# A pair of MLP chunks by seven block products: another order of products and sums, weight mixing begun earlier, a late half of the last DFT, outputs in 128-row pieces

## Chip, cores and metric

One core of a Trainium2 chip runs the kernel. The metric is the device time of one execution in microseconds (us). TensorE (PE) multiplies, VectorE (DVE), ScalarE (ACT) and GpSimd (POOL) do elementwise work, and the queue of SyncE (SP) issues the DMAs. Each engine takes its instructions in program order.

## What is computed

```
x  = attention(q, k, v)          # 8 batches, 32 global rows + 512 local rows (window 32), 8 heads of 64
X  = fft(fft(x, axis=1), axis=2) # 544 rows, 512 columns
u  = x + real(X)
un = (u - mean(u)) / sqrt(var(u) + 1e-6)
y  = u + relu(un @ w_ch1) @ w_ch2     # 512 -> 2048 -> 512
```

Inputs and output are float32. Every float32 operand of a matmul is split into two float16 parts, hi and lo, and the three products hi·hi, hi·lo, lo·hi are summed, so each product of the mathematics is three matmuls on PE.

## The kernel before

**Stages.** The eight batches pass through attention, a DFT (`d_` functions: a first half along the rows, `d_first`, a second half `d_second` by three pieces kt = 0, 1, 2, whose last is the tail of 32 rows, `d_tailsec`; `d_addc`, `d_add`, `d_as`, `d_tadd` add the result to x) and an MLP (`f_` functions). The MLP works on 17 chunks of 256 rows; chunk 16 collects the eight 32-row tails. Chunks 0 to 12 run the plain way, each with 8 steps of `f_first` (first layer into PSUM), `f_hi` and `f_lo` (relu and its two float16 parts) and `f_second` (second layer, summed in PSUM).

**The two pairs.** The last four chunks run as two pairs u = 0 and 1, (13, 14) and (15, 16): `jobs_duo`. For the first layer of a pair the rows of the two chunks and two halves of the 512 inputs and of the hidden columns make 2 by 2 blocks, and seven block products P1 to P7 take the place of eight. The products need sums of blocks of the activations (`s_un`, `s_mix` on DVE, split by `s_hi` on ACT and `s_lo` on DVE, turned by a DMA transpose `s_turn`, groups g = 0 to 3) and sums of blocks of the weights, which POOL makes in eight pieces n (`t_sum` twice, `t_mix`, `t_lo`; `t_hi` is on ACT between the last two). A pair runs in two halves:

- first half, 8 steps s: P1 and P2. `p_copy` takes P1 from PSUM to SBUF (x1), `p_sum` makes c11 = P2 + x1, `p_relu` (ACT) and `p_rest` (DVE) split it, `p_second` multiplies it into the accumulator of the first chunk;
- second half, 8 steps s: P4, P5, P6, P7, P3. `p_copy` takes P4 and P5 to SBUF; then x1 = P6 + x1, u3 = P7 + x1, c12 = x1 + P5, c21 = u3 − P4, c22 = u3 + P5, c12 = P3 + c12, two `p_relu`, two `p_rest`, and two `p_second`: number 2 (c21 and c22, 12 matmuls of 512 columns, second chunk) and number 1 (c12, 6 matmuls, first chunk). PE runs the `p_second` of a step after the five products of the next one.

One product is 6 matmuls of 256 columns in one PSUM bank. Four banks (`bk`) are shared by the products, the DFT and the attention; P1 of the first pair goes to `ps1` instead.

**What sets the order.** `Plan.run` places every job by costs and due times (`add(engine, cost, function, ..., t=due)`) and picks the banks; the program is then emitted in that order, so costs and due times move instructions on all five queues. `T_AT` and `T_PACE` are the due time of weight piece 0 and the distance of the pieces; `BOOST` brings the DFT of the last batch forward by 40.

**Names in the rows.** Second half of a pair: `bk` is a product in PSUM; `msk`, `vN`, `xd`, `xk` hold x1, and `kT` holds u3 (in the first half c11), `ph` holds c12, c21 and c22, `h` and `hb` are the split operands of `p_second`, `un`, `et`, `pg`, `unh` belong to the `s_` functions, `pgr`, `vf`, `tf`, `tq`, `tp` to the `t_` functions, and `ug`, `pe`, `uh` are turned activations.

**End.** `f_end` adds the accumulator into the X tile, one 128-row piece j at a time, and `f_out` writes a chunk: chunks below 16 as one DMA of 256 rows, chunk 16 as two DMAs whose target is 4 by 32 rows.

## Time and profile before

| | us |
|---|---|
| median of 3 runs | 1039.15 (1038.97 to 1042.64) |
| profiled execution | 1041.4 |
| its span | 1039.6 |
| PE busy | 922.8 (89%) |
| DVE busy | 734.4 (71%) |
| ACT busy | 621.6 (60%) |
| POOL busy | 599.8 (58%) |

The profile counts microseconds from the start of the span. A share of busy time is an average over the stages; which engine bounds a stage is read from windows of the trace, from the waits of PE and from the chain of work that ended last. "granted clock" is TensorE's clock as a share of its upper level, 2.4 GHz; 0.50 is its lower level, 1.2 GHz. Mean durations overlap a little between neighbours of one engine: the distance from start to start of two equal DVE instructions is about 0.08 us less than the duration.

### The profile page before, as it was taken

To read this page: it belongs to the slowest core of one execution; us is meant where nothing else is said; L and a number is where in the kernel's file an instruction comes from. 1 tells how busy PE (TensorE), PEld (TensorE's weight loads), DVE (VectorE), ACT (ScalarE), POOL (GpSimd) and SP (SyncE) were. 2 spreads that over 40 slices of the span, in tenths; PEclk is the share of its full clock that TensorE was granted. 3 is DMA by queue.
4 is the path that set the end of the run, shared out by engine and by line. 5 is a ranking of instruction groups with operands and counts; after the bars stand their busy time and mean duration, and the time that the engine had idled before them with its cause. 6 is when DMAs were issued, how large, how long until landed. Compare 5 with 4: busy or idle time off the path is not lost.

```text
span 1039.6 us, 25360 instructions
## 1 busy us (share of the span) xinstructions
PE 922.8 (89%) x9768; PEld 640.7 (62%) x9768; DVE 734.4 (71%) x1929; ACT 621.6 (60%) x1379; POOL 599.8 (58%) x861
## 2 busy tenths in 40 slices
PE   2353558999999999999999999999999998799995
PEld 1243346666777677666766776677676775466662
DVE  4887998977668856785688568867755568984442
ACT  7996777972787388638864885578355334332221
POOL 6999765862686267526854784486246467850000
PEclk9986579999999999999999999999999999899998
DMA  9899356462675286329752874485245114121001
GB/s 361 252 281 239 91 107 135 108 135 42 146 149 116 40 173 133 87 44 170 142 107 55 143 164 75 88 159 94 40 85 79 42 31 85 21 52 41 1 1 41
DMA packets 227761, 113.10 MB, mean 109 GB/s; under 512 B 202776, under 2 KB 210104, under 8 KB 227640
## 3 DMA queue, kind: packets, MB, share of 16 engines
q1 hardware_dynamic: 227640, 111.49, 48.6%
q8 instruction: 76, 1.25, 0.5%
q14 instruction: 45, 0.37, 0.1%
HBM read 47.37 MB, written 9.44 MB: 55 GB/s over the span
## 4 chain that ended last, share of the span: by engine, by line
PE 61%; DVE 7%; DMA 4%; POOL 4%; ACT 3%; issue 1%; SPq 1%; DVEq 0%; POOLq 0%; ACTq 0%
PE ps L1059 20%; PE acc L1078 20%; PE bk L1207 4%; PE ps L1265 3%; PE bk L616 3%; PE acc L1265 2%; DMA pl<-ph 2%; PE bk L940 2%; PE bk L661 1%; PE bk L664 1%; DMA X<-xt 1%; PE bk L905 1%; PE bk L688 1%; PE bk L724 1%; DVE ph L1234 1%
## 5 line engine op out<-in xcount | busy, mean ns | idle before, releaser
L1059 PE MATMUL ps<-uh,wh 128*128 128x256 f16 x2496 | 290.3, 273 | 3.5 <-DVE h L1068 2.7
L1078 PE MATMUL acc<-wh,h 128*128 128x512 f16 x1248 | 286.5, 379 | 1.9 <-DVE h L1068 1.1
L1059 PEld LDWEIGHTS <-wh 128*128 128x128 f16 x2496 | 240.2, 98 | 38.7 <-issue 4.7
L1078 PEld LDWEIGHTS <-h 128*128 128x128 f16 x1248 | 116.3, 98 | 131.0 <-DVE h L1068 2.9
L640 POOL TENSOR_TENSOR ph<-pe,ph 128x448 f16<-128x448 f32 (+1 forms) x128 | 139.0, 1100 | 74.1 <-ACT ph L635 60.9
L1068 DVE SCALAR_TENSOR_TENSOR h<-ps,h 128x512 f16<-128x512 f32 x104 | 71.5, 688 | 117.2 <-ACT h L1064 117.0
L1064 ACT ACTIVATE h<-ps 128x512 f16<-128x512 f32 x104 | 61.5, 592 | 117.6 <-PE ps L1059 116.9
L624 DVE CUSTOM_DVE_ANT_0 pe<-bk,msk,z 128x224 f32<-128x224 f32 (+1 forms) x256 | 102.3, 454 | 19.6 <-PE bk L616 14.5
L631 ACT ACTIVATE pe<-pe,nm 128x224 f32<-128x224 f32 (+1 forms) x256 | 104.8, 475 | 13.0 <-DVE nm L624 12.7
L661 PE MATMUL bk<-vN,pl 128*128 128x65 f16 x768 | 66.5, 200 | 23.7 <-DMA pl<-ph 14.7
L635 ACT ACTIVATE ph<-pe 128x448 f16<-128x448 f32 (+1 forms) x128 | 70.9, 578 | 18.4 <-DMA pl<-ph 17.8
L661 PEld LDWEIGHTS <-pl 128*128 128x128 f16 x768 | 58.7, 103 | 26.0 <-DMA pl<-ph 20.8
L1039 POOL TENSOR_TENSOR ve<-ve 128x2 f32<-128x2 f32 x17 | 4.3, 251 | 102.5 <-DVE un L1019 99.9
L616 PEld LDWEIGHTS <-qT 64*128 64x128 f16 x1536 | 49.8, 98 | 21.4 <-issue 17.9
L664 PEld LDWEIGHTS <-pl 96*128 96x128 f16 (+1 forms) x768 | 56.9, 102 | 10.0 <-issue 6.0
L616 PE MATMUL bk<-kT,qT 64*128 64x192 f16 (+2 forms) x1536 | 57.0, 220 | 6.7 <-POOL kT L600 4.2
L664 PE MATMUL bk<-vB,pl 96*128 96x65 f16 (+1 forms) x576 | 50.9, 201 | 0.0
L1265 PE MATMUL acc<-wh,h 128*128 128x512 f16 x192 | 46.6, 379 | 1.6 <-ACT h L1247 1.0
L600 POOL TENSOR_TENSOR kT<-qk,kT 128x559 f16<-128x559 f32 x32 | 40.6, 1270 | 12.3 <-ACT kT L595 12.1
L431 PE MATMUL wl<-wm,partb 128*128 128x256 bf16 x64 | 18.4, 390 | 32.8 <-DVE wm L421 32.8
L575 POOL TENSOR_TENSOR vN<-vf,vN 128x640 f16<-128x640 f32 x32 | 44.5, 1393 | 4.3 <-ACT vN L571 4.0
L1265 PE MATMUL ps<-wh,hb 128*128 128x512 f16 x192 | 45.2, 385 | 1.2 <-DVE hb L1252 1.2
...
## 6 DMA issues: line engine op xcount, KB each, us to landing
...
pl<-ph SPq DMA_TRANSPOSE x128, 3.3
```

What stands on the lines that cost most here:

```text
L616: nc.tensor.matmul(S[h][:, t + w0:t + w1], qT[r, a, j], kT[r, k0:k0 + w1 - w0], start=m == 0, stop=m == 2)
L624: nc.vector.tensor_tensor_reduce(self.per[j][:, h, 0:w], S[h][:, t:t + w], self.msk[:, j, 0:w], z[:, 8:9], 3e38, op0=ALU.add, op1=ALU.min, ...
L631: self.nc.scalar.activation(pe[:, h], pe[:, h], AF.Exp, bias=nm[:, h:h + 1], scale=-1.0)
L635: self.nc.scalar.activation(ph[:, 0, :, 0:WIDE[i % 4]], self.per[i % 4][:, :, 0:WIDE[i % 4]], AF.Copy)
L640: self.nc.gpsimd.tensor_sub(ph[:, 1, :, 0:w], self.per[i % 4][:, :, 0:w], ph[:, 0, :, 0:w])
L661: nc.tensor.matmul(pv[:, j % 2, h], pl[:, 4 * a + 2 * h], vN[:, j, c, h, :], start=m == 0, stop=False)
L664: nc.tensor.matmul(pv[:, j % 2, h], pl[0:n, 4 * a + 2 * h + 1], vb, start=False, stop=m == 2)
L1059: nc.tensor.matmul(ps[:, q], wt[:, w, c0:c0 + P], uh[:, :, 4 * a + kt, :], start=n == 0, stop=n == 11)
L1064: self.nc.scalar.activation(h[:, 0], self.fps[c, fp], AF.Relu)
L1068: self.nc.vector.scalar_tensor_tensor(h[:, 1], self.fps.pop((c, fp)), 0.0, h[:, 0], op0=ALU.max, op1=ALU.subtract)
L1078: nc.tensor.matmul(self.acc_f[c][j], h[:, a, q, j * P:(j + 1) * P], self.w[1, f][:, w, :], start=f == 0 and a == 0 and w == 0, stop=f == 1 ...
L1265: nc.tensor.matmul(self.acc_f[c][j], h[:, a, q, j * P:(j + 1) * P], self.w[1, f][:, w, :], start=first and q + a + w == 0, stop=last and q ...
```

## The change

1. **Sums.** The order of products in the second half is P6, P7, P5, P4, P3 (for s = 7: P6, P7, P5, P3, P4). `p_copy` of P4 and P5 is gone: c12 = P5 + x1, c22 = P5 + u3 and c21 = u3 − P4 each take one operand from PSUM. In s = 7 `p_second` 1 stands before `p_second` 2.
2. **Weight pieces.** `T_AT` is 808 in place of 826, `T_PACE` 9.0 in place of 7.5; the planner's costs of `t_sum`, `t_mix`, `t_hi`, `t_lo` are larger.
3. **Last batch.** `BOOST` no longer holds for the second DFT half of pieces kt = 1 and 2 and what follows them (`d_second`, `d_addc`, `d_add` of kt = 1, `d_tailsec`, `d_as`, `d_tadd`).
4. **Outputs.** `p_out` writes the 128-row piece j of a chunk right after its `f_end`; chunk 16 keeps its two DMAs to 4 by 32 rows.
5. **Order of groups and costs.** For j = 1 the groups are made in the order 1, 2, 3 in place of 3, 1, 2; the planner's costs of `s_un`, `s_mix`, `s_lo`, `p_sum`, `p_rest`, `p_relu`, `d_addc`, `d_add` are larger.

No matmul is added or removed. The planner's order is the same on all queues until late in batch 7 (PE's row 15,729 of 19,466).

```diff
-T_AT, T_PACE = 826.0, 7.5
+T_AT, T_PACE = 808.0, 9.0
...
+    def p_out(self, c, j):
+        b, k = divmod(c, 2)
+        to = self.out[b, 256 * k + P * j:256 * k + P * j + P, :] if b < B else self.out[4 * j:4 * j + 4, SL:T, :]
+        self.nc.sync.dma_start(to, self.u_row(c, j))
...
     def p_copy(self, u, s, n):
-        self.nc.scalar.activation(self.p_bufs(s)[{"P1": "x1", "P4": "c21", "P5": "c22"}[n]], self.pb[u, s, n], AF.Copy)
+        self.nc.scalar.activation(self.p_bufs(s)["x1"], self.pb[u, s, n], AF.Copy)
...
-        (ve.tensor_sub if o == "c21" else ve.tensor_add)(v[o], a, v[b])
+        if o == "c21":
+            ve.tensor_sub(v[o], v[b], a)
+        else:
+            ve.tensor_add(v[o], a, v[b])
...
-            add("POOL", 2.6, self.t_mix, n, r=[("qT", "T", n, 0), ("qT", "T", n, 1)], w=[tw], t=T + 3)
-            add("ACT", 1.1, self.t_hi, n, r=[tw, *done.get(n, [])], w=[home], t=T + 5)
+            add("POOL", 3.4, self.t_mix, n, r=[("qT", "T", n, 0), ("qT", "T", n, 1)], w=[tw], t=T + 3)
+            add("ACT", 1.25, self.t_hi, n, r=[tw, *done.get(n, [])], w=[home], t=T + 5)
...
-            add("DVE", 1.35, self.s_mix, u, j, r=un, w=[mix, ("sm", 0)], t=L, back=False)
-            for g in (3, 1, 2):
+            add("DVE", 2.5, self.s_mix, u, j, r=un, w=[mix, ("sm", 0)], t=L, back=False)
+            for g in ((1, 2, 3) if j else (3, 1, 2)):
...
-            b = prod(s, "P4", t)
-            add("ACT", .36, self.p_copy, u, s, "P4", r=[b, *end], w=[cw, R], t=-1e3, back=False)
-            b = prod(s, "P5", t)
-            add("ACT", .36, self.p_copy, u, s, "P5", r=[b, *end], w=[cz], k=[R], t=-1e3, back=False)
             b = prod(s, "P6", t)
             summ(s, "x1", "P6", "x1", [b, x1], [x1], xk)
             b = prod(s, "P7", t)
-            summ(s, "u3", "P7", "x1", [b, x1], [u3, ("xu", u, s)], xk)
-            summ(s, "c12", "x1", "c22", [x1, cz], [c12], [R, *xk], .34)
-            b = prod(s, "P3", t)
-            summ(s, "c21", "u3", "c21", [u3, cw], [cw], [R, ("xu", u, s)], .34)
-            summ(s, "c22", "u3", "c22", [u3, cz], [cz], [R, ("xu", u, s)], .34)
-            split(s, 2, .58, [cw, cz], [R], ("pl", "s", u, s), [f, f + 2], t + 1.5 * STEP + 2)
-            summ(s, "c12", "P3", "c12", [b, c12], [c12], [R])
-            split(s, 1, .36, [c12], [R], ("h", "s", u, s, 1), [f + 2], t + 1.5 * STEP + 1)
+            summ(s, "u3", "P7", "x1", [b, x1, *end], [u3, xu], xk)
+            b = prod(s, "P5", t)
+            summ(s, "c12", "P5", "x1", [b, x1, *end], [c12, R], xk)
+            summ(s, "c22", "P5", "u3", [b, u3], [cz], [R, xu])
+            for n in ("P3", "P4") if s == 7 else ("P4", "P3"):
+                b = prod(s, n, t)
+                if n == "P4":
+                    summ(s, "c21", "P4", "u3", [b, u3], [cw], [R, xu])
+                    split(s, 2, .60, [cw, cz], [R], ("pl", "s", u, s), [f, f + 2], t + 1.5 * STEP + 2)
+                else:
+                    summ(s, "c12", "P3", "c12", [b, c12], [c12], [R])
+                    split(s, 1, .40, [c12], [R], ("h", "s", u, s, 1), [f + 2], t + 1.5 * STEP + 1)
...
-            add("SP", .39, self.f_out, c, r=[("uj", c, 0), ("uj", c, 1)], w=[("out", c)], k=[("X", c // 2)], svc=3.2, t=T, back=False)
+                add("SP", .39, self.p_out, c, j, r=[("uj", c, j)], w=[("out", c, j)], k=[("X", c // 2)], svc=1.6, t=T, back=False)
...
-            if j.fn.__name__.startswith("d") and j.a[0] == B - 1:
+            n = j.fn.__name__
+            if n.startswith("d") and j.a[0] == B - 1 and not (n in ("d_second", "d_addc", "d_add") and j.a[1] or n in ("d_tailsec", "d_as", "d_tadd")):
                 j.t -= BOOST
```

**Place 1: DVE, first pair, second half, step s = 2** (`vN` holds x1, `kT_63` u3, `ph` c12, c21, c22; in the changed kernel the sums have lines 1240 and 1242, `p_rest` 1260). Before:

```order
L1234 TENSOR_TENSOR vN<-bk_124,vN 128x256
L1234 TENSOR_TENSOR kT_63<-bk_125,vN 128x256
L1234 TENSOR_TENSOR ph<-vN,ph 128x256
L1234 TENSOR_TENSOR ph<-kT_63,ph 128x256 x2
L1234 TENSOR_TENSOR ph<-bk_122,ph 128x256
L1134 TENSOR_SCALAR un<-X,ve 128x512
L1252 SCALAR_TENSOR_TENSOR hb<-ph,hb 128x512
L1252 SCALAR_TENSOR_TENSOR h<-ph,h 128x256
```

After, from the sums of step s = 1 that still stand ahead of it:

```order
L1240 TENSOR_TENSOR ph<-kT_64,bk_123 128x256
L1242 TENSOR_TENSOR ph<-bk_122,ph 128x256
L1165 TENSOR_TENSOR unh<-un,unh 128x512
L1260 SCALAR_TENSOR_TENSOR hb<-ph,hb 128x512
L1260 SCALAR_TENSOR_TENSOR h<-ph,h 128x256
L1242 TENSOR_TENSOR vN<-bk_125,vN 128x256
L1242 TENSOR_TENSOR kT_63<-bk_124,vN 128x256
L1242 TENSOR_TENSOR ph<-bk_123,vN 128x256
L1242 TENSOR_TENSOR ph<-bk_123,kT_63 128x256
L1240 TENSOR_TENSOR ph<-kT_63,bk_122 128x256
L1242 TENSOR_TENSOR ph<-bk_125,ph 128x256
```

Three sums of a step had both operands in SBUF and now read a bank; the last sum of s = 2 reads bank 125 again, which its first sum (`vN<-bk_125`) sets free.

**Place 2: DVE, first pair, first half, steps s = 0 to 2** (`kT` holds c11, the last name on the right is x1). Before, from `f_end` of chunk 12 on, is the same chain of `kT<-bk` and `h<-kT` with two banks; after:

```order
L1083 SCALAR_TENSOR_TENSOR X<-acc_13167,ve,X 128x512
L1242 TENSOR_TENSOR kT_63<-bk_122,msk 128x256
L1165 TENSOR_TENSOR unh<-et,unh 128x512
L1260 SCALAR_TENSOR_TENSOR h<-kT_63,h 128x256
L1242 TENSOR_TENSOR kT_64<-bk_122,msk 128x256
L1134 TENSOR_SCALAR un<-X,ve 128x512
L1260 SCALAR_TENSOR_TENSOR h<-kT_64,h 128x256
L1165 TENSOR_TENSOR unh<-pg,unh 128x512
L1242 TENSOR_TENSOR kT_63<-bk_122,vN 128x256
L1141 TENSOR_TENSOR et<-un 128x256
```

P2 of the steps s = 0 to 4 goes to bank 122 alone, because the other three hold results of the last DFT half until `d_addc`, `d_add` and `d_tadd` of batch 7, which now stand behind s = 3, s = 5 and later.

**Place 3: ACT, first pair, `t_hi` of weight piece 4** (`vf<-pgr` and `vf<-vf`; `ph<-bk` is the removed copy of P4, `xk<-ps` the copy of P1 of s = 5). Before:

```order
L1161 ACTIVATE unh<-pg 128x512
L1229 ACTIVATE ph<-bk_122 128x256
L1124 ACTIVATE vf<-pgr 128x512
L1124 ACTIVATE vf<-vf 128x512
L1161 ACTIVATE unh<-un 128x512
L1229 ACTIVATE ph<-bk_124 128x256 x2
L1247 ACTIVATE hb<-ph 128x512
```

After:

```order
L1255 ACTIVATE h<-kT_64 128x256
L1161 ACTIVATE unh<-pg 128x512
L1124 ACTIVATE vf<-pgr 128x512
L1124 ACTIVATE vf<-vf 128x512
L1234 ACTIVATE xk<-ps_13835 128x256
L1255 ACTIVATE h<-kT_63 128x256
L1234 ACTIVATE xk<-ps_13866 128x256
```

The piece moves from the second half into the first one, ahead of the copy of P1 of step s = 5 and of the relu of s = 4.

## Rows read from the trace of the kernel before

**Rows 1.** Windows: length, busy PE, PEld, DVE, ACT, POOL, granted clock, DMA share, GB/s.

```profile
800.00:855.00 55.00, 55.00 (x460) 37.66 (x458) 31.55 (x70) 18.33 (x39) 28.18 (x37) 1.00 0.20 37
855.00:875.00 20.00, 19.40 (x135) 12.85 (x134) 19.18 (x41) 9.14 (x23) 13.97 (x32) 1.00 0.39 70
875.00:932.00 57.00, 47.41 (x285) 29.40 (x284) 51.20 (x87) 19.54 (x44) 43.96 (x59) 0.91 0.24 50
932.00:1027.10 95.10, 95.10 (x635) 61.93 (x633) 41.32 (x100) 23.23 (x56) 0.00 (x0) 1.00 0.04 13
```

**Rows 2.** Waits of PE from 830 on: waiter, releaser, us in total, times, longest.

```profile
PE bk L1207 <- ACT ph L1229: 4.1, 3, 2.6
PE bk L1207 <- DMA pe<-unh: 2.1, 1, 2.1
```

**Rows 3.** Chain that ended last, two steps of the second pair: start, us, what.

```profile
988.04 3.28 PE bk L1207 x30
...
995.20 3.27 PE bk L1207 x30
```

**Rows 4.** Windows of 1 us, columns as in the first group.

```profile
886.00:887.00 1.00, 1.00 (x7) 0.69 (x6) 1.00 (x3) 0.20 (x1) 1.00 (x2) 0.50 0.00 0
```

**Rows 5.** Timeline of DVE, second half of the first pair: start, us, instruction.

```profile
887.81 2.25 DVE L1234 TENSOR_TENSOR ph<-kT,ph 128x256 f32<-128x256 f32 x2
889.98 0.41 DVE L1234 TENSOR_TENSOR ph<-bk,ph 128x256 f32<-128x256 f32 x1
...
905.22 0.75 DVE L1234 TENSOR_TENSOR ph<-kT,ph 128x256 f32<-128x256 f32 x2
```

**Rows 6.** Groups by line from 830 on: count, busy us, mean ns, idle before.

```profile
L1234 DVE TENSOR_TENSOR ph<-kT,ph 128x256 f32<-128x256 f32 x32 | 15.5, 525 | 0.0
L1252 DVE SCALAR_TENSOR_TENSOR hb<-ph,hb 128x512 f16<-128x512 f32 x16 | 12.0, 748 | 3.6 <-ACT hb L1247 3.6
L1229 ACT ACTIVATE ph<-bk 128x256 f32<-128x256 f32 x32 | 11.8, 379 | 27.7 <-PE bk L1207 27.7
L1252 DVE SCALAR_TENSOR_TENSOR h<-ph,h 128x256 f16<-128x256 f32 x16 | 7.8, 485 | 0.0
L1234 DVE TENSOR_TENSOR ph<-bk,ph 128x256 f32<-128x256 f32 x16 | 6.7, 418 | 0.0
L1165 DVE TENSOR_TENSOR unh<-un,unh 128x512 f16<-128x512 f32 (+1 forms) x8 | 6.5, 810 | 2.0 <-ACT unh L1161 1.8
L1151 DVE TENSOR_SCALAR un<-X,ve 128x512 f32<-128x512 f32 x4 | 2.6, 652 | 0.1
L1012 DVE TENSOR_SCALAR ve<-ve 128x2 int32<-128x2 int32 x3 | 1.9, 630 | 0.1
```

**Rows 7.** Timeline of POOL: start, us, instruction, idle before it and releaser.

```profile
838.71 1.15 POOL L1129 TENSOR_TENSOR tq<-pgr,tq 128x512 f16<-128x512 f32 x1 [15.43 <-ACT tq L1124]
...
863.34 0.31 POOL L1039 TENSOR_TENSOR ve<-ve 128x2 f32<-128x2 f32 x1 [1.74 <-DVE un L1134]
...
872.38 0.73 POOL L1115 TENSOR_TENSOR pgr<-tf 128x256 f32<-128x256 f32 x1
...
920.00 1.60 POOL L1129 TENSOR_TENSOR tp<-vf,tp 128x512 f16<-128x512 f32 x1
```

**Rows 8.** The end: timelines of PE, DVE and SP, then windows of 0.5 us.

```profile
1026.26 1.46 PE L1265 MATMUL acc<-wh,h 128*128 128x512 f16 x6
1027.19 1.41 DVE L1083 SCALAR_TENSOR_TENSOR X<-acc,ve,X 128x512 f32<-128x512 f32 x2 [4.71 <-PE acc L1265]
1028.52 1.40 DVE L1083 SCALAR_TENSOR_TENSOR X<-ps,ve,X 128x512 f32<-128x512 f32 x2
...
1029.29 1.37 SPq L1092 DMA_DIRECT2D out<-X  x2
...
1030.00:1030.50 0.50, 0.00 (x0) 0.00 (x0) 0.00 (x0) 0.00 (x0) 0.00 (x0) 1.00 1.03 385
...
1034.00:1034.50 0.50, 0.00 (x0) 0.00 (x0) 0.00 (x0) 0.00 (x0) 0.00 (x0) 0.50 0.25 98
```

More of the change, by code (lines that the diff above doesn't have):

```diff
@@ L1501, in jobs_mixes @@
             for o in range(2):
-                add("POOL", 1.16, self.t_sum, n, o, r=[self.whobj[0, 4 * (kt + 2 * o) + c], *late], w=[("qT", "T", n, o)], t=T, hold=T)
+                add("POOL", 1.2, self.t_sum, n, o, r=[self.whobj[0, 4 * (kt + 2 * o) + c], *late], w=[("qT", "T", n, o)], t=T, hold=T)
             tw = ("tw", n)
-            add("POOL", 2.6, self.t_mix, n, r=[("qT", "T", n, 0), ("qT", "T", n, 1)], w=[tw], t=T + 3)
-            add("ACT", 1.1, self.t_hi, n, r=[tw, *done.get(n, [])], w=[home], t=T + 5)
-            add("POOL", 2.4, self.t_lo, n, r=[tw, home], w=[home], t=T + 7)
+            add("POOL", 3.4, self.t_mix, n, r=[("qT", "T", n, 0), ("qT", "T", n, 1)], w=[tw], t=T + 3)
+            add("ACT", 1.25, self.t_hi, n, r=[tw, *done.get(n, [])], w=[home], t=T + 5)
+            add("POOL", 2.5, self.t_lo, n, r=[tw, home], w=[home], t=T + 7)
     def jobs_duo(self, add, u):
@@ L1525, in jobs_duo @@
             un, ve, hl, L0 = ("un", "pre", u, j), ("ve", A), ("unh", "pre", u, j), L - 10
-            add("DVE", .58, self.s_pre, u, j, r=[("uj", A, j), ve, *first], w=[un], k=[("X", A // 2)], t=L0, back=False)
+            add("DVE", .66, self.s_pre, u, j, r=[("uj", A, j), ve, *first], w=[un], k=[("X", A // 2)], t=L0, back=False)
             add("ACT", .55, self.s_hi, u, j, 0, r=[un], w=[hl], t=L0, back=False)
@@ L1533, in jobs_duo @@
             for n, c in enumerate(PAIRS[u]):
-                add("DVE", .58, self.s_un, u, j, n, r=[("uj", c, j), ("ve", c), *first], w=[un[n]], k=[("X", c // 2)], t=L, back=False)
+                add("DVE", .66, self.s_un, u, j, n, r=[("uj", c, j), ("ve", c), *first], w=[un[n]], k=[("X", c // 2)], t=L, back=False)
             mix = ("et", "s", u, j)
-            add("DVE", 1.35, self.s_mix, u, j, r=un, w=[mix, ("sm", 0)], t=L, back=False)
-            for g in (3, 1, 2):
+            add("DVE", 2.5, self.s_mix, u, j, r=un, w=[mix, ("sm", 0)], t=L, back=False)
+            for g in ((1, 2, 3) if j else (3, 1, 2)):
                 src = un[1:2] if g == 3 else [mix, ("sm", 0)]
@@ L1542, in jobs_duo @@
                 add("ACT", .55 if wide else .35, self.s_hi, u, j, g, r=([mix] if g < 3 else []) + src, w=[hl], t=L, back=False)
-                add("DVE", .70 if wide else .42, self.s_lo, u, j, g, r=([mix] if g < 3 else []) + src + [hl], w=[hl], t=L, back=False)
+                add("DVE", .90 if wide else .56, self.s_lo, u, j, g, r=([mix] if g < 3 else []) + src + [hl], w=[hl], t=L, back=False)
                 home = (f"w{12 + u}", "s") if g == 3 else ("eh", "s") if (u, g) == (1, 1) else ("us", u, g)
@@ L1580, in jobs_duo @@
             summ(s, "c11", "P2", "x1", [b, x1, *end], [c11], own)
-            split(s, 0, .36, [c11], [], ("h", "s", u, s, 0), [f], t + STEP / 2 + 1)
+            split(s, 0, .41, [c11], [], ("h", "s", u, s, 0), [f], t + STEP / 2 + 1)
         for s in range(8):
@@ L1585, in jobs_duo @@
             x1, u3, cw, cz, c12 = ob(s)
[L1586 to L1589 removed]
+            xu = ("xu", u, s)
             b = prod(s, "P6", t)
```

6 lines of the change are left out of this document (3 added, 3 removed).

## Prediction

> **What bounds the kernel now.** I read the windows by stage first. In 800 to 855 and in 932 to 1027.1 PE is busy throughout at granted clock 1.00 [rows 1]: work saved there on another engine brings nothing. All the loss lies between. PE idles 0.60 us in 855 to 875 and 57.00 − 47.41 = 9.59 us in 875 to 932, 10.2 in all, and in the second of these the mean granted clock is 0.91 [rows 1]. Single windows there stand at 0.50 [rows 4], the lower level, so about (1 − 0.91) · 57 / 0.5 = 10.3 us pass at it. With PE busy in 8.5 of them, as its share of this stage suggests, that is 8.5 / 2 = 4.3 us of lost work. Together 14.5 us is an estimate of what a perfect overlap of this stage would give back; should PE have been busier than that, up to 16.
>
> Who makes PE wait there is shown by two views. The waits of PE name only 6.2 us: 4.1 on ACT's copy of a product, since the bank isn't free before it, and 2.1 on a turned activation [rows 2]. The windows show the cause behind: DVE is busy 51.2 of 57 us [rows 1]. Its timeline shows why: two sums with both operands in SBUF take 2.25 us at 887.81, while POOL works, and 0.75 at 905.22, while it doesn't; the sum that reads a bank takes 0.41 between them [rows 5]. By the group means the same three kinds are 525 and 418 ns [rows 6]. So DVE is the bound of the first pair's second half, partly because POOL mixes weights until 920.00 + 1.60 = 921.6 [rows 7].
>
> **Sums.** Per step three sums go from SBUF to PSUM operands. By the means that is 3 · (525 − 418) = 0.3 us a step; in the two steps that fall into POOL's work it is 3 · (1.12 − 0.41) = 2.1 a step. First pair: two steps at 2.1, six between 0 and 0.3, about 4 to 5 us of DVE's 51.2. The 32 copies, 11.8 us of ACT [rows 6], vanish, and with them PE's 4.1 us wait on them. In their place banks are freed by DVE's sums, so PE now waits on DVE's queue directly. In the second pair PE has no gap [rows 1], so nothing is gained there; a step lasts 995.20 − 988.04 = 7.16 us [rows 3], and DVE's work of a step, six sums at 0.42, hb 0.75 and h 0.49 [rows 6], is 3.8 us, so the extra dependence costs nothing either.
>
> **Weight pieces.** Before, POOL stood 15.43 us until 838.71 for ACT's `t_hi` of piece 0 [rows 7]. The order now puts that `t_hi` ahead of this idle time. POOL's last `t_lo` ended at 921.6; 15.4 earlier is 906, and of the 20 − 13.97 = 6.0 us that it idles in 855 to 875 [rows 1], waiting for ACT and DVE, most should go too, since ACT is rid of the copies: 900, between 896 and 906. What it gives is that DVE's two-operand work after 900 runs at undisturbed durations; what it costs is in place 3: `t_hi` 4 now stands on ACT ahead of the copy of P1 of s = 5 and of the relu of s = 4. POOL's `t_mix` 4 begins after the roots, which took 9.04 us [rows 7]; started some 9 us earlier they let `t_mix` 4 end at about 868, so that relu is about 0.5 us late (0 to 2.5, should the roots start as late as before).
>
> **Last batch.** The late results of the second DFT half hold three of four banks, so P2 of s = 0 to 4 cycles through bank 122 alone. A first-half step has 12 product matmuls at 3.28 / 30 = 0.109 us and 6 wide ones. The rest of a second-half step, (7.16 − 3.28) / 18 = 0.216 each, gives 1.31 + 1.29 = 2.6 us a step [rows 3]. P2 of the next step comes 2.6 us after this one; c11 is 0.42 [rows 6], so a wait arises only if DVE is over 1.5 us late. DVE's queue in the eight steps: 8 · (0.42 + 0.49) = 7.2 for c11 and h, eight DFT additions which I take at 0.42 like the sums, 3.4, five `s_lo` at 0.81 = 4.1, and about 3.5 for one `s_un` and one `s_mix` (bounded by five instructions at 0.41 and at 1.12, which is 2.1 and 5.6), 18.2 in 20.8 us of PE. Neighbours overlap by 0.08, 31 times, 2.5 us: 15.7. That fits, but not with much room where POOL is busy. I take 1.4 us of loss for this half, 0.5 to 4.
>
> **Second half of the first pair.** The critical place is step s = 1, where `l_v`, a group's `s_un` and the tail's `d_tadd` stand in one step (place 1). DVE there: sums, four whole ones and two late ones, 2.2; hb 0.75, h 0.49, `s_lo` 0.81, `s_un` 0.65, `l_v` up to three times 0.63, 1.9, and the tail's four at 0.42, 1.7 [rows 6]: 8.5 us. The means hold both busy and idle POOL. With 0.7 more (1.12 − 0.41, what POOL adds to a sum) for each of hb, h and `s_lo` it is 10.6. I take 9.2, nearer the means, since POOL rests between its instructions; PE's work of a step is 7.16 [rows 3], so 2.0 us remain, which PE sees as a wait at the P3 of s = 2, since its bank is freed by the first sum of s = 2, queued behind `s_lo` and both `p_rest` of s = 1. Bounds 0 (should DVE be ahead of PE when s = 1 begins) and 3.5 (10.6 − 7.16). From s = 2 on the load is 3.8 plus one `s_lo` and one `s_un`, 5.3, and falls; the second half recovers. The granted clock after that one wait: nothing up to 4 us, I take 1. The 2.1 us wait for a turned activation should go, because the groups are made in the order in which they are needed. Left over: 1.4 + 2.0 + 1.0 = 4.4 of 14.5, a gain of 10.1.
>
> **The tail.** PE's last matmuls end at 1026.26 + 1.46 = 1027.72, and the span 11.9 us later at 1039.6. Before, `f_end` of chunk 15 (1027.19) and 16 (1028.52) follow each other on DVE, and both DMAs of chunk 16 are issued at 1029.29 [rows 8], 1.57 after PE's end, behind chunk 15's data: the window at 1030 moves 385 GB/s at DMA share 1.03, that of 1034 only 98 at 0.25 [rows 8]. So chunk 16's DMAs flow on a quarter of the engines and decide the end; their shape stays as it is. In the changed order `p_second` 1 of s = 7 stands first, so `f_end` of chunk 15 runs under `p_second` 2, and the first piece of chunk 16 is ready about when its first half of the wide matmuls is done. I put its issue at 0.4 before PE's end instead of 1.57 after, and the second piece's at 1.0 after. The two share the same few engines, so the end moves by between 1.3 (the second piece decides) and 2.0 (the flow begins 1.97 earlier). Chunk 15's data goes out of its way too, which may bring up to 3.5. I take 2.0.
>
> **Sum.** 10.1 + 2.0 = 12.1 from the profiled execution's 1041.4, which is 1029.3. The median of the runs is 1039.15, 2.25 below that execution, so I expect 1027.
>
> **Rivals.**
>
> All of the loss goes. If DVE is 1.5 us ahead of PE when s = 1 begins and that step takes 8.5, and the one-bank loop costs nothing, 14.5 + 2 go: 1041.4 − 16.5 − 2.25 = 1022.6; with 16 in place of 14.5, 1021. Against it: one engine takes the sums, the freeing of banks and the group work.
>
> DVE stays the bound in s = 1. Should each of hb, h and `s_lo` wait for a whole instruction of POOL, 1.15 to 1.60 us [rows 7], the step is 8.5 + 3 · 1.5 = 13 us. The stall is then 5.8, the granted clock costs about 3 (before, 10.2 us of idle went with 4.3), and 1.4 stay from the first half: 10.2 left over, a gain of 4.3 + 2, hence 1033. For it: 2.25 for two sums, twice 1.12. Against it: that is 0.75 more for each, not 1.5, and hb's mean of 0.75 leaves no room for it.
>
> The Trainium skill says, on the page "SBUF — State Buffer", section "Who interferes with whom", that a DVE instruction with two SBUF inputs and a GpSimd instruction that reads SBUF lock each other out for a whole instruction. By that rule this rival would be the likely one, and the time 1033; the 0.41 of the sum from PSUM beside the 1.12 agrees with its direction, and the 0.75 instead of 1.5 speaks against its full length.
>
> It changes nothing. The sums freed on ACT and DVE are given back by the one-bank loop, by later `t_hi` and by waits on DVE for banks in each of the eight second-half steps (about 1.5 each, 12 in all, and 2 by the clock), 14 of 14.5: 1041.4 − 2.5 − 2.25 = 1036.7. For it: the banks are freed by one engine alone. Against it: a step's own DVE work is 3.8 of 7.16.
>
> Slower. The one-bank loop of the first half becomes the bound: the next P2 waits for c11, c11 waits in DVE's queue behind a DFT addition, `s_lo` or `s_mix`, while POOL is busy. If each of eight steps waits 1 us (8 us), the granted clock falls for half of that stage (10 us of work at half speed: 10 more), and 5 us of the second half's waits stay, 23 are lost where 14.5 were: 1041.4 + 8.5 − 2 − 2.25 = 1045.6. Without the fall of the clock it takes (16.5 − 5) / 8 = 1.4 us a step to lose the whole gain, and more than 2 for a measurable loss. For it: PE is at 1.00 in this stage now with 0.60 us idle [rows 1], so there is a lot to lose. Against it: 15.7 us of DVE in 20.8.
>
> **Chances.** Forecast 0.63 (its own range 1022.5 to 1031.5, from the bounds of the four terms), all gone 0.11, DVE still the bound 0.15, no change 0.05, slower 0.06. The range, 1021 to 1034.5, holds the first three but for their outer ends and leaves out about 0.2. Faster or slower by over 0.5% (about 5 us: what a measurement of this kernel can tell from no change) means below 1034 or above 1044.3: faster 0.63 + 0.11 + 0.11 = 0.85, within 0.04 + 0.05 = 0.09, slower 0.06.
>
> **What would show it.** Right: between 875 and 932 PE's idle time falls below 4 us and the granted clock above 0.97; the three sums stay near 0.42 while POOL works; POOL's last `t_lo` ends near 898; PE's only longer wait is at the P3 of s = 2, on DVE; from PE's end to the span's it is about 10 us. Wrong: PE idle in 855 to 875 at each P2 (the one-bank loop), `p_second` of s = 4 over 1 us late behind `t_hi` 4, hb over 1.5 us in s = 1, or chunk 16's DMA ending as late after PE as before.

## The result, and the profile after

The changed kernel takes 1025.81 us (median of 4 runs, 1025.38 to 1028.04), the kernel before 1039.06 (4 runs, 1037.91 to 1042.64): ratio 0.9871, 95% interval 0.9843 to 0.9899. Forecast were 1027 us and a range of 1021 to 1034.5.

The two profiled executions differ by 15.5 us (spans 1039.6 and 1024.1), and not all of that is the change. Up to an instruction of DVE late in batch 7 both kernels run the same instructions in the same order; its start shows how much of the difference was there already. First the row of before, then that of after (timeline of DVE: start, us, instruction):

```profile
763.18 0.42 DVE L677 TENSOR_TENSOR X<-bk,dn 128x256 f32<-128x256 f32 x1
```

```profile
759.77 0.42 DVE L677 TENSOR_TENSOR X<-bk,dn 128x256 f32<-128x256 f32 x1
```

So 3.4 us lie in the shared part, by which the profile of before came late (the forecast took off 2.25 for that, from the median). From this row to PE's end, called **the stretch** below, it was 1027.72 − 763.18 = 264.5 us before and is 1014.84 − 759.77 = 255.1 after: 9.5 less. From PE's end to the span's end it was 11.9 and is 9.3: 2.6 less. Together 12.1, which is the sum of the forecast (10.1 + 2.0), with its two terms each half a microsecond off. The windows of the whole stretch, first before, then after (start:end, length, busy PE, PEld, DVE, ACT, POOL, granted clock, DMA share, GB/s):

```profile
763.18:1027.72 264.54, 254.35 (x2024) 167.32 (x2022) 163.69 (x366) 94.20 (x214) 110.15 (x153) 0.98 0.20 39
```

```profile
759.77:1014.84 255.07, 250.13 (x2024) 166.54 (x2021) 166.43 (x368) 84.07 (x182) 110.50 (x153) 0.99 0.20 42
```

PE runs the same 2024 matmuls in both. It idled 10.2 us and idles 4.9, so 5.3 of the 9.5 us are idle time. The other 4.2 are time in which PE was busy, for the larger part because more of its work ran at the lower clock before.

The windows by stage of after (columns as above), to be held against [rows 1]:

```profile
800.00:855.00 55.00, 54.36 (x447) 38.05 (x446) 43.01 (x75) 19.90 (x43) 42.25 (x54) 1.00 0.15 37
855.00:875.00 20.00, 18.24 (x124) 11.62 (x122) 16.30 (x33) 8.63 (x21) 18.51 (x30) 1.00 0.35 73
875.00:932.00 57.00, 54.46 (x358) 35.67 (x357) 46.24 (x102) 14.50 (x28) 23.76 (x41) 0.97 0.14 32
```

POOL's 44.0 us in the last of these windows became 23.8, and 28.2 in the first became 42.3: its work went to where PE loses 0.6 us. PE's idle time in 875 to 932 fell from 9.6 to 2.5; in 855 to 875 it rose from 0.6 to 1.8. The waits of PE from 780 on (waiter, releaser: us in total, times, longest):

```profile
PE bk L1207 <- DVE xt L980: 2.5, 1, 2.5
PE acc L1273 <- DVE h L1260: 0.9, 2, 0.7
PE acc L1273 <- ACT h L1255: 0.8, 1, 0.8
PE bk L1207 <- DVE kT L1242: 0.6, 1, 0.6
```

ACT's copies and the turned activation of [rows 2] are gone from the list. One longer wait is left, and the clock falls right behind it, but only until 892.1 (windows of 1 us, columns as above):

```profile
888.00:889.00 1.00, 0.21 (x2) 0.15 (x2) 0.97 (x3) 0.00 (x0) 1.00 (x2) 0.83 0.00 0
889.00:890.00 1.00, 1.00 (x6) 0.71 (x5) 1.00 (x3) 0.78 (x2) 0.79 (x2) 0.50 0.28 66
```

What DVE does ahead of that wait is step s = 1 of the second half, with POOL at work (timeline of DVE):

```profile
879.86 0.41 DVE L1242 TENSOR_TENSOR msk<-bk,msk 128x256 f32<-128x256 f32 x1
...
882.07 1.08 DVE L1012 TENSOR_SCALAR ve<-ve 128x2 int32<-128x2 int32 x1
...
884.29 1.34 DVE L1151 TENSOR_SCALAR un<-X,ve 128x512 f32<-128x512 f32 x1
885.66 1.27 DVE L977 TENSOR_TENSOR xt<-xt,asm 32x256 f32<-32x256 f32 x1
886.86 0.94 DVE L978 TENSOR_TENSOR xt<-xt,asm 32x256 f32<-32x256 f32 x1
...
888.76 0.42 DVE L1240 TENSOR_TENSOR ph<-kT,bk 128x256 f32<-128x256 f32 x1
...
891.28 0.41 DVE L1242 TENSOR_TENSOR vN<-bk,vN 128x256 f32<-128x256 f32 x1
```

Sums that read a bank take 0.41 to 0.43 whatever POOL does. Most of what reads SBUF alone is stretched, down to operations on two columns that take 1.08. Below, these are compared with the same instructions without POOL's reads.

### The profile page after: what moved, and what is told of

Same layout as the page of the kernel before. It is cut to its first block, busy times and chain, and to the rows that moved or that the text cites. A ratio compares the mean times of both kernels' runs of the same rounds, so it can differ in the third digit from the quotient of the medians.

```text
span 1024.1 us, 25350 instructions
## 1 busy us (share of the span) xinstructions
PE 920.3 (90%) x9768; PEld 641.4 (63%) x9768; DVE 733.5 (72%) x1929; ACT 611.5 (60%) x1347; POOL 599.1 (59%) x861
## 5 line engine op out<-in xcount | busy, mean ns | idle before, releaser
L1255 ACT ACTIVATE hb<-ph 128x512 f16<-128x512 f32 x16 | 10.1, 630 | 62.8 <-DVE ph L1240 62.8
```

## The experiments

In the kernels whose names begin with u_ one part of the change is undone, in those with only_ one part alone is made in the kernel before. In those with cut POOL's mixing is left out. Those with v_ are attempts at a better kernel. Since the shared part came between 759.8 and 765.0 us in the profiles of these kernels, the parts are judged by the stretch, and by the time from PE's end to the span's end. Both are read from one profile of each kernel, and how much the stretch varies from profile to profile of one kernel wasn't measured; the intervals of the ratios, about 3 us on either side, can't tell stretches apart that differ by 1 us or less. Each ratio is to the kernel before as it ran beside that kernel (medians 1039.06 to 1041.7), so the ratios compare better than the medians.

| kernel | stretch, us | PE's end to span's end | median | ratio to before (95%) |
|---|---|---|---|---|
| before | 264.5 | 11.9 | 1039.06 | |
| after | 255.1 | 9.3 | 1025.81 | 0.9871 (0.9843 to 0.9899) |
| u_sums | 255.5 | 9.3 | 1027.25 | 0.9875 (0.9859 to 0.9892) |
| u_weights | 265.3 | 9.3 | 1036.82 | 0.9975 (0.9957 to 0.9993) |
| u_late | 261.0 | 9.3 | 1033.73 | 0.9945 (0.9924 to 0.9966) |
| u_out | 254.5 | 11.9 | 1032.27 | 0.9922 (0.9899 to 0.9945) |
| only_sums | 264.3 | 11.9 | 1040.23 | 0.9989 (0.9976 to 1.0001) |
| only_weights | 255.1 | 11.9 | 1032.33 | 0.9917 (0.9886 to 0.9947) |
| b_cut | 249.1 | 11.9 | | |
| a_cut | 247.7 | 9.3 | | |
| w_cut | 253.6 | 9.3 | | |
| l_cut | 251.3 | 9.3 | | |
| v_tail16 | 252.8 | 4.4 | 1022.88 | 0.9820 (0.9796 to 0.9845) |
| v_lean16 | 256.0 | 4.5 | 1024.72 | 0.9852 (0.9830 to 0.9875) |

**u_sums**, the sums of before in the steps s = 0 to 6:

```diff
+            if s < 7:
+                b = prod(s, "P4", t)
+                add("ACT", .36, self.p_copy, u, s, "P4", r=[b, *end], w=[cw, R], t=-1e3, back=False)
+                b = prod(s, "P5", t)
+                add("ACT", .36, self.p_copy, u, s, "P5", r=[b, *end], w=[cz], k=[R], t=-1e3, back=False)
...
+                summ(s, "c12", "x1", "c22", [x1, cz], [c12], [R, *xk], .40)
```

> The changed kernel with the sums of before in the steps s = 0 to 6 of the second half: P4 and P5 copied by ACT, three sums per step with both operands in SBUF, order P4, P5, P6, P7, P3; s = 7 and all else as changed. Theory (sums taken from PSUM carry most of the gain, because DVE's sums with two SBUF operands cost about 1.1 us while POOL mixes and 0.4 otherwise): in s = 0 and 1 the DVE has about 2 us a step more, PE's idle time between 855 and 932 grows by 3 to 5 us and more time passes at the lower clock, the median is 1029.5 to 1033. Rival (DVE has slack now that POOL ends earlier): within 1 us of the changed kernel's 1025.8.

Measured: a stretch of 255.5, 0.4 more than after, and the same ratio. The median, 1027.25, lies between the two ranges, nearer the rival's. PE idles 6.4 us from 800 to 932, 1.4 more than in after, but behind a wait of 2.6 us as long as there the clock didn't fall this time, and PE is busy 1.0 less. The theory that the sums carry most of the gain falls; by the ratio and the stretch the rival holds.

**u_weights**, the weight pieces of before:

```diff
-T_AT, T_PACE = 808.0, 9.0
+T_AT, T_PACE = 826.0, 7.5
...
-            add("POOL", 3.4, self.t_mix, n, r=[("qT", "T", n, 0), ("qT", "T", n, 1)], w=[tw], t=T + 3)
+            add("POOL", 2.6, self.t_mix, n, r=[("qT", "T", n, 0), ("qT", "T", n, 1)], w=[tw], t=T + 3)
```

> The changed kernel with due times and costs of the weight pieces as before (826, 7.5). Theory (the earlier mixing takes POOL out of the way of DVE's two-operand work): POOL's last t_lo ends about 20 us later than 897, hb, h and s_lo of the steps s = 1 to 4 stay near twice their undisturbed time, the median is 1028 to 1031. Rival 1 (only the sums mattered): 1025 to 1027. Rival 2 (t_hi of piece 4, which now stands in front of the relu of s = 4, costs more than the early mixing gives): 1023 to 1025, and the 1 us gap of PE at p_second of s = 4 is gone.

Measured: 265.3, 10.2 more than after, which is more than the theory's upper end. PE's two longest waits:

```profile
PE bk L1207 <- DMA ug<-unh: 4.5, 1, 4.5
PE bk L1207 <- DVE kT L1242: 3.4, 1, 3.4
```

The second wait, in the first half, is at the P2 of s = 1, the one-bank loop: DVE comes 3.4 us late to c11, and the granted clock falls behind it (0.83 in the mean of 855 to 875). The first, 4.5 us until 890.2, is in the second half, for a turned group. So it isn't only the steps s = 1 to 4 that suffer, as the theory had it, but the first half too.

**u_late**, the second DFT half of the last batch as early as before:

```diff
-            if n.startswith("d") and j.a[0] == B - 1 and not (n in ("d_second", "d_addc", "d_add") and j.a[1] or n in ("d_tailsec", "d_as", "d_tadd")):
+            if n.startswith("d") and j.a[0] == B - 1:
```

> The changed kernel with the second DFT half of the last batch as early as before. Theory (the later half moves DVE work out of the queue just ahead of the second half's first sums, at the price of one bank for P2): without it the idle time of 0.6 us at P2 of s = 1 is gone, but the DFT additions and the variance stand ahead of the first sums of the second half; 1027 to 1030. Rival (the one-bank loop and the late tail cost more than that, since the one wait of 2.54 us of the changed kernel is for the tail's bank): 1022 to 1025.

Measured: 261.0, 5.9 more than after. The direction is the theory's, the size above it, and the place another: the wait for c11 in the first half doesn't go but grows to 2.9 us (at the P2 of s = 2), and PE waits for turned groups 3.7 us once and 1.2 us twice.

**u_out**, outputs and s = 7 as before:

```diff
-            for n in ("P3", "P4") if s == 7 else ("P4", "P3"):
+            for n in ("P4", "P3"):
...
-                add("SP", .39, self.p_out, c, j, r=[("uj", c, j)], w=[("out", c, j)], k=[("X", c // 2)], svc=1.6, t=T, back=False)
+            add("SP", .39, self.f_out, c, r=[("uj", c, 0), ("uj", c, 1)], w=[("out", c)], k=[("X", c // 2)], svc=3.2, t=T, back=False)
```

> The changed kernel with one output DMA per chunk behind both f_end as before for chunks 13 to 15 (chunk 16 two DMAs), and p_second 2 before p_second 1 in s = 7. Theory (the tail alone gave 2.6 us, from 11.9 to 9.3 us between PE's end and the end of the span): about 11.9 us from PE's end to the span's end, the median 1027.9 to 1029. Rival (PE's last stage hides the change, or the DMA of chunk 16 takes what it takes): 1025.5 to 1026.5.

Measured: 11.9 us from PE's end to the span's, as the theory has it. In the stretch nothing is lost. The median is above the theory's range. In the profiled execution the shared part ends at 764.98, 5.2 us later than in after, which would account for that; whether it was as late in the other executions isn't shown.

**only_sums**, the first part of the change in the kernel before:

```diff
-            b = prod(s, "P4", t)
-            add("ACT", .36, self.p_copy, u, s, "P4", r=[b, *end], w=[cw, R], t=-1e3, back=False)
...
+            summ(s, "c22", "P5", "u3", [b, u3], [cz], [R, xu])
```

> The kernel before with the first part of the change alone: order P6, P7, P5, P4, P3 in all steps, no copies of P4 and P5, all sums from PSUM. Measured from a DVE instruction in the part that all kernels share (the last but one X<-bk,dn, which starts at 763.18 before and at 759.77 in the changed kernel) to PE's end, before takes 264.5 us and the changed kernel 255.1. First theory (the sums relieve the engine that bounds the stage): 258 to 261. Second theory, after the run without the sums (they matter only where POOL mixes, and the waits move to the next DVE instruction that reads two SBUF operands): 262.5 to 265, time within 0.3% of before.

Measured: 264.3, ratio 0.9989 (0.9976 to 1.0001). The second theory's numbers hold: 32 copies and three sums a step from SBUF are gone, and the time is the same. DVE does get work taken off, but PE has nothing of it. Windows of 82 us, up to about the end of the first pair and beginning 90 us behind the row of the shared part, first before, then only_sums (columns as above):

```profile
853.18:935.18 82.00, 71.81 (x455) 45.86 (x454) 73.61 (x137) 29.44 (x68) 59.67 (x93) 0.94 0.27 53
```

```profile
850.69:932.69 82.00, 71.64 (x456) 45.84 (x455) 71.00 (x139) 26.37 (x56) 58.81 (x93) 0.94 0.26 53
```

DVE is busy 2.6 us less, PE as long as before. PE's waits on ACT's copies [rows 2] are replaced by waits on DVE, whose first sum of a step now frees the bank (`xd`, `vN`):

```profile
PE bk L1207 <- DMA pe<-unh: 2.9, 1, 2.9
PE bk L1207 <- DVE xd L1237: 2.6, 1, 2.6
PE bk L1207 <- DVE vN L1237: 2.1, 1, 2.1
```

**b_cut and a_cut**, the mixing left out in the kernel before and in the changed one, every other instruction in its place:

```diff
-        self.nc.gpsimd.tensor_add(f.rearrange("p a c -> p (a c)"), w[:, 0], w[:, 1])
+        self.nc.gpsimd.memset(f.rearrange("p a c -> p (a c)"), 0.0)
...
-        ve.tensor_sub(a[:, 0], f[:, 1], f[:, 0])
+        ve.memset(a[:, 0], 0.0)
...
-            self.nc.gpsimd.tensor_sub(t[:, 1, 2 * i:2 * i + 2], v, t[:, 0, 2 * i:2 * i + 2])
+            self.nc.gpsimd.memset(t[:, 1, 2 * i:2 * i + 2], 0.0)
```

> The kernel before with POOL's mixing of the weight blocks left out: t_sum, t_mix and t_lo fill their tiles with a constant and read nothing, every other instruction and its order is as before. Contention theory (DVE's two-operand work is stretched by POOL's reads, and that is most of the loss between 855 and 932): PE idles less than 3 us there instead of 10.2, the granted clock stays at 1.00, and the stretch of 264.5 us becomes 250 to 253. Rival (the order on DVE, the copies on ACT and the banks make the waits): PE still idles over 6 us, the stretch is 259 to 263.

> The changed kernel with POOL's mixing left out in the same way. Contention theory: the waits of 0.66 and 0.29 us on h in the first half go, the wait of 2.54 us for the bank of the tail shrinks under 0.7, no fall of the clock; the stretch of 255.1 us becomes 250 to 252. Rival (that wait is made by the number of DVE instructions ahead of it): the wait stays over 1.5 us, the stretch is over 253.

These kernels leave the weight sums out, and each was run once. Measured: 249.1 and 247.7, both below the theory's ranges. The windows of b_cut, the order of before (columns as above):

```profile
855.00:875.00 20.00, 19.99 (x137) 13.18 (x135) 17.83 (x44) 11.61 (x28) 12.59 (x41) 1.00 0.39 79
875.00:932.00 57.00, 55.78 (x375) 36.59 (x375) 38.88 (x98) 20.13 (x46) 15.31 (x46) 1.00 0.24 49
```

PE idles 1.2 us in place of 10.2, and the granted clock stays at its upper level. In a_cut it doesn't idle at all (window of the stretch):

```profile
763.69:1011.40 247.71, 247.71 (x2024) 165.95 (x2022) 147.94 (x368) 84.26 (x182) 68.23 (x153) 1.00 0.21 44
```

So 247.7 is the stretch without loss: before lost 16.8 us, after loses 7.4. Of the 16.8, 15.4 go with the mixing: DVE's 51.2 us in [rows 1] become 38.9 in the same order. The same step as above in a_cut (timeline of DVE):

```profile
882.14 0.17 DVE L1012 TENSOR_SCALAR ve<-ve 128x2 int32<-128x2 int32 x1
...
882.54 0.55 DVE L1151 TENSOR_SCALAR un<-X,ve 128x512 f32<-128x512 f32 x1
883.12 0.42 DVE L977 TENSOR_TENSOR xt<-xt,asm 32x256 f32<-32x256 f32 x1
```

1.08 against 0.17, 1.34 against 0.55, 1.27 against 0.42: each of these instructions loses 0.8 to 0.9 us. POOL's fills don't do that. This instruction of DVE in a_cut has both operands in SBUF:

```profile
867.46 0.68 DVE L1165 TENSOR_TENSOR unh<-pg,unh 128x512 f16<-128x512 f32 x1
```

and POOL fills all that time (timeline of POOL in a_cut):

```profile
867.38 0.31 POOL L1118 MEMSET vf<- 128x256 f32 x1
867.63 0.99 POOL L1108 MEMSET tf<- 128x512 f32 x2
```

Its 0.68 is what it takes alone. So it is with the three others of that kind between 863.7 and 869.6, where POOL fills without a pause (`unh` 0.69 at 864.62, `h` 0.42 at 865.23 and 868.06). So the rows put the stretching of DVE's instructions down to POOL's reads.

The fills are also shorter than the mixing (0.31 against 0.73 for 256 columns), and with that a second way goes by which the mixing reached PE: ACT stood for POOL's `t_mix`, with a relu and copies queued behind. Before, at `t_hi` of piece 4 (timelines of ACT and DVE):

```profile
874.69 0.63 ACT L1124 ACTIVATE vf<-pgr 128x512 f16<-128x512 f32 x1 [2.24 <-POOL pgr L1117]
...
876.79 0.43 DVE L1252 SCALAR_TENSOR_TENSOR h<-kT,h 128x256 f16<-128x256 f32 x1 [1.58 <-ACT h L1247]
```

ACT stands 2.24 us for POOL there and 5.43 at piece 5; DVE's `h` and the `s_lo` behind it come late, and behind these PE waits 1.0 for the relu, 2.1 for a turned activation and 0.8 for a copy of P4 or P5. In b_cut no `t_hi` waits for POOL. So the 15.4 us are what the mixing costs by its reads and by its length together. DVE's 12 us speak for the reads as the larger share, but no run took one away without the other.

**w_cut and l_cut**, the same in the order of u_weights and of u_late, with the edits shown there and here:

> The changed kernel with the weight pieces' due times and costs of before (its stretch was 265.3 us, 10.2 more than the changed kernel) and POOL's mixing left out; the order on DVE, ACT and PE is that of the run u_weights. Contention theory (the later mixing cost those 10 us by stretching DVE's work in and ahead of the pair): 250 to 254. Rival (what costs is the other order that the planner makes, with the DFT and the group work ahead of the first P2): the wait of 3.45 us at the second P2 stays over 2 us and the stretch is over 257.

> The changed kernel without the later second DFT half (its stretch was 261.0, 5.9 more than the changed kernel, with waits of 2.9 us for c11 at the second P2 and of 3.7 and 2.3 us for turned groups), and with POOL's mixing left out as in the other runs of that kind. Contention theory: all of that is DVE work stretched by POOL, the stretch becomes 248 to 250. Rival (part of it is the order: the DFT additions and the variance stand ahead of the groups): a wait of over 2 us for a turned group stays, 251 to 255.

Measured: 253.6 and 251.3, the theory's range for w_cut and the rival's for l_cut. Of the 17.6 us lost in u_weights 11.7 go with the mixing, of the 13.3 in u_late 9.7. The rest stays without it, so it is put down to the order: a turned group comes late even without POOL's mixing.

```profile
PE bk L1207 <- DMA ug<-unh: 2.7, 1, 2.7
```

This is PE's longest wait in w_cut. Before and after don't have this wait for `ug`; in l_cut it is 2.2.

**only_weights**, the second part of the change in the kernel before:

```diff
-T_AT, T_PACE = 826.0, 7.5
+T_AT, T_PACE = 808.0, 9.0
...
-            add("ACT", 1.1, self.t_hi, n, r=[tw, *done.get(n, [])], w=[home], t=T + 5)
+            add("ACT", 1.25, self.t_hi, n, r=[tw, *done.get(n, [])], w=[home], t=T + 5)
```

> The kernel before with the second part of the change alone: T_AT, T_PACE and the planner's costs of t_sum, t_mix, t_hi and t_lo. Its stretch before is 264.5 us, with POOL's mixing left out 249.1, the changed kernel's 255.1. Contention theory, with the sums worth little by themselves: POOL is done by 900, the stretch becomes 256 to 259, faster than before by 0.5 to 0.9%. Rival (the parts only work together, since the run without the late half lost 5.9 us): 261 to 264, within 0.4%.

Measured: 255.1, a little better than the theory's 256 to 259, and faster by 0.8%: this part alone has all of the stretch's gain. The windows of only_weights:

```profile
800.00:855.00 55.00, 55.00 (x462) 38.61 (x458) 42.46 (x76) 19.77 (x43) 41.54 (x53) 1.00 0.14 32
855.00:875.00 20.00, 17.63 (x115) 10.49 (x113) 19.63 (x35) 7.80 (x22) 18.32 (x31) 1.00 0.38 85
875.00:932.00 57.00, 53.43 (x362) 35.12 (x361) 47.81 (x99) 20.13 (x45) 26.05 (x43) 1.00 0.21 44
```

13 us of POOL's work went into 800 to 855, where DVE now has 42.5 us in place of 31.6 [rows 1] and PE still idles nowhere. In 855 to 875 PE idles 2.4 us, 1.8 more than before.

**v_tail16**, the tail of the last DFT half early, chunk 16 in DMAs of 32 rows on two queues:

```diff
-(n in ("d_second", "d_addc", "d_add") and j.a[1] or n in ("d_tailsec", "d_as", "d_tadd")):
+(n in ("d_second", "d_addc", "d_add") and j.a[1]):
...
-        self.nc.sync.dma_start(to, self.u_row(c, j))
+        for i in range(4):
+            (self.nc.sync, self.nc.scalar)[i % 2].dma_start(self.out[4 * j + i, SL:T, :], x[32 * i:32 * i + 32])
```

> The changed kernel with two edits that show in separate places. First, the tail piece of the last DFT half and its additions keep their early place (only d_second, d_addc and d_add of kt = 1 are late). Theory: PE's wait of 2.54 us for the tail's bank is gone and with it the fall of the clock, the stretch of 255.1 becomes 251.5 to 253.5; rival: the four DVE operations of the tail in the first half, stretched by POOL, make P2 wait in its one-bank loop, 255 to 257. Second, chunk 16 is written by eight DMAs of 32 rows, on SP's and ACT's queues in turn, instead of two of 4 by 32 rows. Theory: its 512 KB flow on all 16 engines at 385 GB/s (1.4 us instead of 5.1), and from PE's end to the span's it takes 5.5 to 6.5 us instead of 9.3; rival: the issues, about 0.9 us each, take as long, 8.5 or more. By both theories the median is 1018 to 1021.

Measured: 252.8, PE's wait for the tail's bank 0.4 in place of 2.5, no fall of the clock: the theory. From PE's end to the span's end 4.4 us, better than expected. The median, 1022.88, is over its range; the shared part ends 4.7 us later in this profile than in after, and whether that holds for the other executions isn't shown. It has the best ratio of the study. A window of 0.5 us at its end (columns as above):

```profile
1019.50:1020.00 0.50, 0.00 (x0) 0.00 (x0) 0.00 (x0) 0.00 (x0) 0.00 (x0) 1.00 0.98 246
```

against one of after:

```profile
1019.00:1019.50 0.50, 0.00 (x0) 0.00 (x0) 0.00 (x0) 0.00 (x0) 0.00 (x0) 0.50 0.26 102
```

**v_lean16**, the weights, the sums and the outputs of v_tail16 in the kernel before, without the later DFT half, the order of groups and the other costs. Against the changed kernel:

```diff
-            add("DVE", 2.5, self.s_mix, u, j, r=un, w=[mix, ("sm", 0)], t=L, back=False)
-            for g in ((1, 2, 3) if j else (3, 1, 2)):
+            add("DVE", 1.35, self.s_mix, u, j, r=un, w=[mix, ("sm", 0)], t=L, back=False)
+            for g in (3, 1, 2):
```

> The kernel before with the weight pieces' due times and costs, the sums from PSUM with s = 7 in the new order, and outputs by 128 rows with chunk 16 as eight DMAs of 32 rows on two queues; without the later half of the last DFT, without the other order of groups and without the other changed costs of DVE's operations. The weight pieces alone gave 255.05 us for the stretch, the whole change 255.07. Theory (with POOL done earlier the sums that still meet its reads, 2.58 us for three in s = 0, shorten DVE's queue, while the later half only repays what the changed costs do to the groups): 252 to 254, and 4.4 us from PE's end to the span's, median 1018 to 1021, at or below 1022.9. Rival (the sums are worth nothing here either, the wait only moves): 254.5 to 256, median 1021 to 1023.

Measured: 256.0, at the rival's upper end; the median, 1024.72, is above both ranges. Against only_weights it has the sums in addition and is no faster in the stretch (256.0 and 255.1). What becomes of the sums' saving is seen in DVE's timeline. In only_weights, at s = 2, two sums from SBUF take long, and `p_rest` behind them doesn't:

```profile
894.63 1.81 DVE L1234 TENSOR_TENSOR ph<-kT,ph 128x256 f32<-128x256 f32 x2
...
897.17 0.69 DVE L1252 SCALAR_TENSOR_TENSOR hb<-ph,hb 128x512 f16<-128x512 f32 x1
897.77 0.42 DVE L1252 SCALAR_TENSOR_TENSOR h<-ph,h 128x256 f16<-128x256 f32 x1
```

In v_lean16 the same two sums take 0.41 each, and `p_rest` of the same step takes 1.22 and 1.37:

```profile
895.06 0.41 DVE L1246 TENSOR_TENSOR ph<-bk,kT 128x256 f32<-128x256 f32 x1
895.39 0.41 DVE L1244 TENSOR_TENSOR ph<-kT,bk 128x256 f32<-128x256 f32 x1
...
897.03 1.22 DVE L1264 SCALAR_TENSOR_TENSOR hb<-ph,hb 128x512 f16<-128x512 f32 x1
898.17 1.37 DVE L1264 SCALAR_TENSOR_TENSOR h<-ph,h 128x256 f16<-128x256 f32 x1
```

POOL mixes at 897 in v_lean16 and stands in only_weights. In this step `p_rest` loses what the sums save. In s = 0 it loses less: the three sums save 1.35 us there, and `p_rest` takes 2.41 in place of 2.04. In all, DVE is busy 70.6 us in v_lean16 and 72.2 in only_weights (the 82 us as in only_sums), so more than half of the saving stays on DVE. PE has nothing of the rest either: it no longer waits for `hb` (1.5 in only_weights), but 3.7 us for banks that DVE's sums free, where it was 1.8.

## Why the prediction was right

**The bound.** Right in the main: DVE, because POOL mixes. The estimate of the loss, 14.5 and up to 16, was 16.8 by the run without the mixing; the term that was too small is the clock's, 4.3: PE's own work took 254.35 − 247.71 = 6.6 us longer. The 10.3 us at the lower level make up to 5.1 of that; the rest isn't traced. One reading was wrong: the waits of PE name 9.9 us, not only 6.2. The rest are 2.7 on DVE (`hb`, `ph`, `h`) and 1.0 on ACT's relu, behind `t_hi` 4: that POOL also holds up PE through ACT wasn't seen in the kernel before.

**Luck in the sum.** The loss was put 2.3 us too low (14.5 for 16.8), and what would be left of it 3.0 too low (4.4 for 7.4). In the gain, 10.1 for 9.5, the two all but cancel. That the size came out so well is luck; that the time falls, and through DVE and POOL, isn't.

**Sums.** Here a step of the working fails. It took 4 to 5 us off DVE and PE's 4.1 us on the copies out of the waits, as if both were gained. Alone the sums give 0.3 us of the stretch, left out they cost 0.4, and v_lean16, which adds them to the weights, has 1.0 more than the weights alone: nothing that these runs can tell from zero. The durations were right (0.41 to 0.43 beside POOL). But DVE is relieved by only 1.6 to 2.6 us (only_sums 2.6, u_sums 2.1, v_lean16 1.6), because in part the next instruction that reads SBUF meets POOL's reads instead, as the last two fences of the experiments show for s = 2. And PE doesn't gain the rest, because its waits on the copies (4.1, and 1.0 on DVE for banks) became waits on DVE for banks, 5.2 in all in only_sums. The prediction named this dependence and gave it no price here; its rival "It changes nothing", with a chance of 0.05, describes it, and for the sums by themselves that rival came true.

**Weight pieces.** The prediction let them count only for "DVE's two-operand work after 900" and gave them no term of their own. They are the gain: 9.5 us alone, 10.2 if undone. The prediction has one sum for all parts, so that this error and the one on the sums don't show in the time. The end of POOL's mixing was placed at 900 and is 895.99 + 1.60 = 897.6, or 901.0 on the time scale of before, if both are laid on the row of the shared part (timeline of POOL in after):

```profile
895.99 1.60 POOL L1129 TENSOR_TENSOR tp<-vf,tp 128x512 f16<-128x512 f32 x1
```

**First half.** 1.4 us were forecast; 0.64 (the one-bank loop, at the P2 of s = 1) and 1.76 (p_second of s = 4 and 5) came, within the bounds of 0.5 to 4. Place 3 acted as described, but more strongly. ACT's timeline has it, with the relu of s = 4 as the last row:

```profile
864.71 0.63 ACT L1124 ACTIVATE vf<-pgr 128x512 f16<-128x512 f32 x1 [2.51 <-POOL pgr L1117]
865.85 0.63 ACT L1124 ACTIVATE vf<-vf 128x512 f16<-128x512 f32 x1 [0.51 <-POOL vf L1118]
...
866.65 0.41 ACT L1255 ACTIVATE h<-kT 128x256 f16<-128x256 f32 x1
```

ACT stands 2.5 us for POOL with the relu queued behind, and PE waits 0.81 for that and 0.66 for DVE's `h` behind it. Together that is 1.5 us at `p_second` of s = 4, over the 1 us that the prediction named as a sign of being wrong.

**Step s = 1.** Forecast were 9.2 us of DVE and a stall of 2.0; it took 891.28 − 879.86 = 11.4, and the stall was 2.5. What POOL adds was put on the wrong instructions: on hb, h and `s_lo`, while `l_v`, `s_pre` and the tail's two additions in SBUF were taken at their means. These are the ones that are stretched most (fence of s = 1). hb and h take 0.68 and 0.41 there, for POOL stands from 889.9 to 894.8, waiting for ACT. The place and its reason were others too: P7 of s = 2, the second product of the step, waits for bank 124, which the tail's result holds until `d_tadd`; P3, the last one, doesn't wait for the bank of x1. v_tail16, which frees bank 124 earlier, confirms it. So a stall of nearly the forecast size is luck in part.

**Clock.** 1.0 us forecast; about 3.4 us at the lower level (0.3 of window 888, the three behind it, 0.1 of 892) are up to 1.7 of lost work. u_sums, which has no fall of the clock, has PE busy 1.0 less.

**Last batch.** Taken as a cost with moved work and no gain of its own. Undone it costs 5.9 us, but only_weights and v_lean16, which don't have it either, are within 1 us of after. In the stretch u_late (261.0) and v_lean16 (256.0) differ by nothing but the order of groups and the planner's costs for DVE: these cost 5.0 us where the later half is missing, and the later half repays them. Which of the two, order or costs, wasn't tried apart.

**The tail.** 2.0 forecast (1.3 to 3.5), 2.6 measured, and u_out ties it to the two edits that it undoes, the outputs and the order in s = 7. PE ends at 1012.09 + 2.75 = 1014.84; the first piece of chunk 16 is ready at 1014.41, the second at 1015.63 (timelines of PE and DVE in after):

```profile
1012.09 2.75 PE L1273 MATMUL ps<-wh,hb 128*128 128x512 f16 x12
```

```profile
1013.66 0.75 DVE L1083 SCALAR_TENSOR_TENSOR X<-ps,ve,X 128x512 f32<-128x512 f32 x1 [0.52 <-PE ps L1273]
1014.88 0.75 DVE L1083 SCALAR_TENSOR_TENSOR X<-ps,ve,X 128x512 f32<-128x512 f32 x1 [0.48 <-PE ps L1273]
```

**The rivals.** "DVE stays the bound" was nearer than its chance said: the addition per instruction is up to 0.96 (`h`, 0.42 alone, in the fence here, timeline of DVE in after), not 0.7, though not 1.5 either. That it didn't decide is put down to where the mixing was moved. "Slower" had a mechanism that exists, a late c11 in the one-bank loop: it is 0.64 us here, and 3.4 in u_weights with the clock's fall on top. It wasn't named that the weight pieces decide between the two. The chances have a flaw of their own: the bounds of the four terms, added up, give 1021.7 to 1034.9 and not the forecast's own 1022.5 to 1031.5, so that it overlaps more with its rivals than the chances say.

```profile
869.36 1.38 DVE L1260 SCALAR_TENSOR_TENSOR h<-kT,h 128x256 f16<-128x256 f32 x1
```
